# A fused attention and gated-MLP kernel: clears moved behind the key maximum, an own buffer for the warm-up products, and a fixed table of order and banks

## The chip, the cores and the metric

The kernel runs on one core of a Trainium2 chip. A core has engines that run side by side, each through its own list of instructions in order: TensorE (matmuls and transposes, PE in the profile), ScalarE (ACT), VectorE (DVE), GpSimd (POOL), and SyncE (SP), which issues the transfers. They wait for each other through semaphores. The metric is the device time of one execution in microseconds, the median of the runs; lower is better.

## The reference

One sequence of 2048 rows of 640 numbers goes through a layer norm. From there two branches run: attention with 32 heads of 20 numbers each, and a gated MLP block that shifts quarters of its hidden features along the sequence. The result is the input plus the attention output times the SiLU of the other branch.

```python
def _A_ref(x, wqkv, wo):            # H = 32, Dh = 20
    ...
    scores = jnp.einsum("bhqd,bhkd->bhqk", q, k) * (Dh ** -0.5)
    p = _softmax(scores, axis=-1)
    o = jnp.einsum("bhqk,bhkd->bhqd", p, v)
    ...
def _B_ref(x, w1, w2, w3, w4):
    h = _gelu(_layernorm(x, axis=-1) @ w1)
    ...
    hs = jnp.concatenate([g0, g1, g2, g3], axis=-1) @ w2
    x1 = x + hs
    h2 = _gelu(_layernorm(x1, axis=-1) @ w3) @ w4
    return x1 + h2
x = A_x
xn = _layernorm(x, axis=-1)
s = _A_ref(xn, A_wqkv, A_wo)
g = _silu(_B_ref(xn, B_w1, B_w2, B_w3, B_w4))
return x + s * g
```

## The kernel before

**A program that plans itself.** The code does not write instructions in their final order. It makes a list of tasks: each names an engine, an estimated duration, what it reads and writes, and sometimes a due time. A planner then orders the tasks of each engine. In the kernel before it is a list scheduler (`schedule`): it steps through an estimated time line and picks, for each engine, the ready task with the earliest derived due time. It also hands out PSUM banks and buffers for exponentials (`acq`, `rel`, `choose`). The due times come from `DUE`, a table of offsets. From the order, `plan_sync` works out the semaphore waits, and `emit` writes each engine's list. On the chip each list is fixed and is run strictly in order.

**The opening.** The input is loaded in eight transfers of two 128-row tiles. Each of the 16 tiles is normalised: for some, VectorE computes the statistics (`bn_stats`, L1014, two halves of 320 for each tile), for others ScalarE does so (`ln_tiles_act`, L1046 and L1048). GpSimd takes the power -0.5 of the variance (L1024, L1060). The normalisation itself runs on VectorE or GpSimd (L1029) or, for the tiles with statistics from ScalarE, on ScalarE (L1071) or GpSimd (L1067). `LNA` says how many tiles of each eight go to ScalarE, `POOLN` which tiles GpSimd normalises. TensorE transposes the normalised tiles (L1120), four tiles and one of five column chunks at a time; VectorE (L1130) or ScalarE (L1127) copies the result to `xnT`. `TRA` lists the copies that ScalarE does.

Ahead of that, TensorE runs warm-up products whose result isn't used (`warm`, L981), so that its clock is at full speed when the work comes. They read `QM`, a buffer of query chunks that GpSimd clears first (L947). `NPF` says how many: 34 tasks of four products at the start, 8 more after the first transposes.

**The softmax bound.** Instead of the row maximum, the kernel subtracts a bound for each query. For the first quad of heads it is made in the opening (`prep`): for each of four chunks, the keys are projected, VectorE takes the largest absolute key (L1193), and ScalarE copies the keys out (L1196). From the maximum over all chunks (L1199) a small matrix `Mq` is filled (L1201). The absolute queries (copied at L1165, the sign bit cleared by a bit operation at L1166) times this matrix give the shift (L1174), which is added to the queries, and the result is copied out (L1181, L1185). Only then can the first scores be computed. GpSimd clears the second halves of `KT` and `QT` (L973, L974) for later quads.

**The body.** Eight quads of four heads, and in each of them four chunks of 512 queries, are worked through; for each there are 16 key tiles of 128. TensorE computes scores (L1524 over rows of the array, L1542 over columns), ScalarE exponentiates 1024 of them per partition at a time (L1589), and TensorE multiplies with the values (L1382). To relieve ScalarE, some pairs of key tiles, the *blocks*, are split: half of each tile's heads is exponentiated by VectorE through integer arithmetic on bit patterns (L1616 makes the exponent bits, L1507 makes three shifted copies), which costs TensorE four value products in place of one (L1516). `ND` gives the number of blocks for each quad and chunk, `NR` the key tiles whose scores use rows of the array. Between the scores lie the projections of later heads, the values, and the whole MLP branch (all through `mm_tile`, L797), with evictions on VectorE.

**The tail.** The last chunk of the last quad is done in halves (`last_half`), then the output projection, the product with the gate, and the stores follow.

Of the kernel before, what the change touches and what calls it, by code (L numbers as in the profile page):

```python
# [6 lines left out]
def _log(*a, **k):  # L7
    pass
# [4 lines left out]
class _Heap:  # L13

    @staticmethod
    def heappush(h, item):
        h.append(item)
        i = len(h) - 1
        while i > 0:
            p = (i - 1) >> 1  # L20
            if h[i] < h[p]:
                h[i], h[p] = h[p], h[i]
                i = p
            else:
                break

    @staticmethod
    def heappop(h):
        last = h.pop()
        if not h:  # L30
            return last
        top = h[0]
        h[0] = last
        n = len(h)
        i = 0
        while True:
            l = 2 * i + 1
            r = l + 1
            m = i
            if l < n and h[l] < h[m]:  # L40
                m = l
            if r < n and h[r] < h[m]:
                m = r
            if m == i:
                break
            h[i], h[m] = h[m], h[i]
            i = m
        return top

    @staticmethod  # L50
    def heapify(h):
        n = len(h)
        for s in range(n // 2 - 1, -1, -1):
            i = s
            while True:
                l = 2 * i + 1
                r = l + 1
                m = i
                if l < n and h[l] < h[m]:
                    m = l  # L60
                if r < n and h[r] < h[m]:
                    m = r
                if m == i:
                    break
                h[i], h[m] = h[m], h[i]
                i = m


heapq = _Heap

# [6 lines left out]
class Task:  # L91
    __slots__ = ("id", "eng", "dur", "fn", "reads", "writes", "due", "name",
                 "preds", "succs", "order_preds", "start", "finish", "seq",
                 "signals", "dma_sem", "lat", "pos", "npred", "prio", "is_dma",
                 "acq", "rel", "stream", "sidx", "cls", "nbytes", "mode", "ndma", "tile", "dlat")

    def __init__(self, tid, eng, dur, fn, reads, writes, due, name, lat, is_dma):
# [28 lines left out]
        self.dlat = 0.0  # L126


class Planner:
# [87 lines left out]
    def task(self, eng, dur, fn, reads=(), writes=(), due=None, name="", lat=0.0,  # L217
             is_dma=False, acq=None, rel=None, stream=None, after=(), cls=0, nbytes=0, mode=0, ndma=1, tile=None, dlat=0.0):
# [6 lines left out]
        t.tile = tile  # L225
        t.dlat = dlat
        if is_dma and nbytes:
            t.lat = self.dma_lat0 + nbytes / self.dma_bw + dlat
# [55 lines left out]
    def avail(self, pstate, a):  # L284

        ps = pstate[self.home[a[0]]]
        return min(max(ps[i][0] for i in banks) for _, banks in self.kinds[a[0]])

    def choose(self, pstate, kind, now):

        ps = pstate[self.home[kind]]
        best = None
        for rank, banks in self.kinds[kind]:
            ft = max(ps[i][0] for i in banks)
            if ft <= now + 1e-9 and (best is None or (rank, ft) < best[0]):
                best = ((rank, ft), banks)
        return best[1]

    def schedule(self, verbose=False):
        tasks = self.tasks  # L300
        n = len(tasks)
        for t in tasks:
            t.succs = []
        for t in tasks:
            for p in t.preds:
                tasks[p].succs.append((t.id, True))
            for p in t.order_preds:
                tasks[p].succs.append((t.id, False))
        horizon = 0.0
        for t in tasks:  # L310
            if t.due is not None:
                horizon = max(horizon, t.due)
        for t in reversed(tasks):
            d = t.due if t.due is not None else INF
            for (sid, sync) in t.succs:
                s = tasks[sid]
                sd = s.prio - s.dur - (SYNC_LAT[t.eng] if sync else 0.0) - t.lat
                if sd < d:
                    d = sd
            if d == INF:  # L320
                d = horizon + 1e6
            t.prio = d
        first = {}
        for t in tasks:
            if t.tile is not None:
                first.setdefault(t.tile, t.prio)
                t.prio = min(t.prio, first[t.tile])
        for t in tasks:
            if t.eng == "dve" and t.rel is not None:
                t.cls = -1  # L330
            if t.cls and t.eng in self.strict_engines:
                t.prio = t.prio + t.cls * self.cls_penalty
        npred = [len(t.preds) + len(t.order_preds) for t in tasks]
        ready_time = [0.0] * n
        eng_free = {e: 0.0 for e in ENGINES}
        ready = {e: [] for e in ENGINES}
        for t in tasks:
            if npred[t.id] == 0:
                heapq.heappush(ready[t.eng], (t.prio, t.id))
# [3 lines left out]
        dma_free = 0.0  # L343
        done = 0
        pe_mode = 0
        WINDOW = 48
        while done < n:
            best = None
            for e in ENGINES:
                h = ready[e]  # L350
                if not h:
                    continue
                tf = eng_free[e]
                tmp = []
                cand = None
                early = None
                saved = set()
                k = 0
                while h and k < WINDOW:
                    item = heapq.heappop(h)  # L360
                    tmp.append(item)
                    k += 1
                    t = tasks[item[1]]
                    rt = ready_time[item[1]]
                    if t.acq:
                        if any(a[0] in saved for a in t.acq):
                            continue
                        r0 = rt
                        for a in t.acq:
                            ft = self.avail(pstate, a)  # L370
                            if ft > rt:
                                rt = ft
                            if ft > tf and a[0] in self.saves and r0 <= tf + self.reserve and (self.hard or rt < INF):
                                saved.add(self.saves[a[0]])
                    if rt <= tf + 1e-9:
                        if cand is None:
                            cand = (tf, item)
                        if e != "pe" or not pe_mode or t.mode == pe_mode:
                            if t.mode == pe_mode:
                                cand = (tf, item)  # L380
                            break
                        continue
                    if cand is None and t.cls < 0 and (t.acq or e != "pe") and rt <= tf + self.hold.get(e, 0.0):
                        cand = (rt, item)
                        break
                    if early is None or rt < early[0]:
                        early = (rt, item)
# [214 lines left out]
class Handle:  # L602
    _n = 0
# [1413 lines left out]
```

## Time and profile before

| what | value |
|---|---|
| time, median of 3 runs | 864.06 us (862.28 to 864.19) |
| profiled span | 862.9 us |
| TensorE busy | 813.6 us |
| ScalarE busy | 818.7 us |
| VectorE busy | 723.7 us |
| GpSimd busy | 41.9 us |
| first exponential starts | 39.44 us |
| granted clock of TensorE, mean | 0.996 |

The busy time of an engine counts the instructions it runs, not its waits. In the profile a line such as L1589 stands for the place in the code that made the instruction; a helper like `mm_tile` (L797) stands for many callers. In the groups of instructions, the number after `|` is the busy time and the mean duration of one, and after the second `|` stands the idle time of the engine just ahead of them, with what ended most of it. The chain of waits follows the work that ended last, back from the end of the program, and gives start, duration and place of each piece.

### The profile page before, as it was taken

The page shows a single profiled execution, that of the slowest core. Times are in us where ns is not written, and L with a number is a line of the kernel's source. Part 1 is how long each engine was busy: PE and PEld are TensorE (multiplying, and loading weights), DVE is VectorE, ACT ScalarE, POOL GpSimd, SP SyncE. Part 2 cuts the span into 40 slices and gives each one's busy share as a digit, 9 for nine tenths or more (in the row PEclk, how much of TensorE's full clock was granted, in tenths as well). Part 3 has the DMA queues.
Part 4 walks back from the last instruction along what each step waited for, and adds up shares of the span by engine and source line. Part 5 has one row for each costly group of instructions (what it writes and reads, how often), then busy time and mean ns, then how long its engine had stood idle before and what let it go on. Part 6 is the DMA issues. An engine that isn't in the chain of part 4 may idle for free.

```text
span 862.9 us, 33979 instructions
## 1 busy us (share of the span) xinstructions
PE 813.6 (94%) x15538; PEld 362.4 (42%) x15538; DVE 723.7 (84%) x977; ACT 818.7 (95%) x855; POOL 41.9 (5%) x74
## 2 busy tenths in 40 slices
PE   6899999999999999999999999999997999999996
PEld 3433433334434533343344444344333444534474
DVE  6728987998998899989887799997986788999765
ACT  6599999999999999999999999999999999999986
POOL 8500000000000100000000000000000000000000
PEclk9999999999999999999999999999999999999999
DMA  7003333313010022223225021323221103032331
GB/s 229 17 9 84 94 114 85 118 28 99 17 56 26 25 59 66 63 74 80 56 69 131 23 71 29 87 64 87 63 55 49 48 25 72 25 103 66 89 114 64
DMA packets 86479, 58.99 MB, mean 68 GB/s; under 512 B 53056, under 2 KB 77840, under 8 KB 86336
## 3 DMA queue, kind: packets, MB, share of 16 engines
q1 hardware_dynamic: 86336, 56.82, 24.3%
q8 instruction: 122, 2.00, 1.0%
q14 instruction: 21, 0.17, 0.1%
HBM read 42.10 MB, written 10.63 MB: 61 GB/s over the span
## 4 chain that ended last, share of the span: by engine, by line
PE 51%; ACT 36%; DVE 10%; DMA 1%; issue 1%; POOL 1%; SPq 0%; DVEq 0%; POOLq 0%
ACT arena L1589 31%; PE psum L797 17%; PE psum L1542 12%; PE psum L1524 7%; PE psum L1382 6%; PE psum L1516 5%; DVE arena L1616 4%; ACT arena L1959 2%; DVE arena L1507 2%; PE psum L981 1%; ACT arena L1888 1%; DMA shifts<-arena 1%; ACT arena L1566 1%; PE psum L1120 1%; DVE arena L1260 1%
## 5 line engine op out<-in xcount | busy, mean ns | idle before, releaser
L1589 ACT ACTIVATE arena<-psum 128x1024 bf16<-128x1024 f32 x786 | 736.2, 1035 | 20.3 <-PE psum L1524 12.9
L797 PE MATMUL psum<-arena 128*32 128x320 bf16 (+1 forms) x5952 | 351.6, 333 | 5.4 <-DVE arena L1216 2.2
L1616 DVE TENSOR_SCALAR arena<-psum 128x1024 uint16<-128x1024 f32 (+1 forms) x222 | 267.8, 1207 | 44.3 <-PE psum L1524 42.8
L1542 PE MATMUL psum<-arena 128*32 128x512 bf16 x3664 | 278.9, 381 | 10.9 <-ACT arena L1589 9.2
L797 PEld LDWEIGHTS psum<-arena 128*32 128x32 bf16 x5952 | 148.0, 96 | 133.2 <-issue 28.8
L1507 DVE TENSOR_SCALAR arena<-arena 128x4096 uint16<-128x4096 uint16 (+1 forms) x174 | 197.4, 1160 | 1.0
L1382 PE MATMUL psum<-arena 128*22 128x512 bf16 x1544 | 148.2, 381 | 2.9 <-ACT arena L1589 2.6
L1516 PE MATMUL psum<-arena 128*22 128x512 bf16 x1760 | 141.2, 380 | 0.7 <-DVE arena L1507 0.4
L1542 PEld LDWEIGHTS psum<-arena 128*32 128x32 bf16 x3664 | 80.0, 95 | 102.4 <-ACT arena L1589 70.4
L1524 PE MATMUL psum<-arena 32*128 32x512 bf16 x1068 | 111.1, 384 | 12.1 <-ACT arena L1589 6.0
L1524 PEld LDWEIGHTS psum<-arena 32*128 32x128 bf16 x1068 | 28.3, 91 | 121.2 <-ACT arena L1589 74.0
L1382 PEld LDWEIGHTS psum<-arena 128*22 128x22 bf16 x1544 | 38.5, 91 | 60.1 <-issue 16.8
L1516 PEld LDWEIGHTS psum<-arena 128*22 128x22 bf16 x1760 | 42.9, 92 | 48.1 <-issue 8.4
L1260 DVE CAST arena<-psum 128x512 bf16<-128x512 f32 x40 | 27.2, 684 | 17.4 <-PE psum L797 17.3
L1955 DVE CAST arena<-psum 128x512 bf16<-128x512 f32 x48 | 32.8, 684 | 4.4 <-PE psum L797 4.4
L1739 DVE SCALAR_TENSOR_TENSOR arena<-psum,arena 128x320 bf16<-128x320 f32 x32 | 15.5, 486 | 18.9 <-PE psum L797 18.9
L1321 DVE CAST arena<-psum 128x320 bf16<-128x320 f32 x32 | 15.4, 488 | 18.2 <-PE psum L797 18.0
L1014 DVE BATCH_NORM_STATS2 arena<-arena 128x6 f32<-128x320 bf16 x52 | 23.0, 478 | 2.7 <-DMA arena<-in_A_x_dram 2.6
L1959 ACT ACTIVATE arena<-arena 128x12288 bf16<-128x12288 bf16 x2 | 20.9, 10446 | 0.0
L1651 DVE COPY arena<-psum 128x512 f32<-128x512 f32 x28 | 19.1, 683 | 0.7 <-PE psum L1516 0.6
L981 PE MATMUL psum<-arena 128*32 128x512 bf16 x168 | 12.8, 463 | 7.3 <-POOL arena L947 6.4
L1664 DVE TENSOR_TENSOR arena<-arena 128x512 bf16<-128x512 f32 x28 | 19.1, 681 | 0.5 <-DMA arena<-recips 0.5
(119 smaller groups left out, 352.1 us busy)
## 6 DMA issues: line engine op xcount, KB each, us to landing
arena<-in_B_w_dram SPq DMA_DIRECT2D x48, 160.0 KB, 2.7
arena<-recips SPq DMA_DIRECT2D x28, 256.0 KB
arena<-arena SPq DMA_DIRECT2D x124, 32.0 KB, 1.9
arena<-in_B_w_dram SPq DMA_DIRECT2D x4, 960.0 KB, 7.0
arena<-in_A_x_dram SPq DMA_DIRECT2D x8, 320.0 KB, 5.3
arena<-in_A_x_dram SPq DMA_DIRECT2D x16, 160.0 KB, 2.4
out_dram<-arena SPq DMA_DIRECT2D x16, 160.0 KB, 1.8
arena<-keys SPq DMA_DIRECT2D x28, 80.0 KB
```

The source lines that it names most:

```text
L797: ins = e.matmul(pb[32 * c:32 * c + 32, 0:N], lhsT(k, c), rhs(k, c), start=(k == 0), stop=(stop and k == nk - 1), tile_position=(0, 32 * c))
L1014: lambda e, li=li, n=n, hh=hh: e.bn_stats(st[:, li, 6 * hh:6 * hh + 6], xn[:, n, hD * hh:hD * hh + hD]),
L1260: T("dve", c_dve(512), lambda e, h=h, c=c: e.tensor_copy(KS[:, 512 * c:512 * c + 512], self.wbank(h)[:, 0:512]), reads=[wa], writes=[A("KS ...
L1382: ins = e.matmul(pb[32 * i:32 * i + 22, 0:512], VA[:, ql, kts[i // 2], i, :], PT[:, slots[i // 2][0].slot, 512 * (i % 2):512 * (i % 2) + 512],
L1507: T("dve", c_dve(w, "4x"), lambda e, v=v, dst=dst: e.tensor_scalar(dst, U[:, ub, 0:w], EXP_B[v], None, op0=ALU.add), reads=halves, writes= ...
L1516: ins = e.matmul(pb[32 * i:32 * i + 22, 0:512], wv, dst[:, at:at + 512].bitcast(BF16), start=first, stop=final, tile_position=(0, 32 * i))
L1524: return e.matmul(out, self.KT[32 * i:32 * i + 32, b, 128 * kt:128 * kt + 128], self.QT[32 * i:32 * i + 32, b, 512 * qc:512 * qc + 512], s ...
L1542: ins = e.matmul(out[32 * c:32 * c + 32, :], self.KT[:, b, 128 * kt + 32 * c:128 * kt + 32 * c + 32], self.QM[:, gb, 2 * a + jj, :], start ...
L1589: lambda e: e.activation(self.PT[:, hp.slot, :], self.psum[:, 512 * hs.slot:512 * hs.slot + 1024], AF.Exp, scale=cfg.scale),
L1616: ins = e.tensor_scalar(U[:, ub, 1024 * at + 512 * k:1024 * at + 512 * k + w], self.psum[:, 512 * hd.slots[k]:512 * hd.slots[k] + w], a_ex ...
L1955: T("dve", c_dve(512), lambda e, h=h, fc=fc, i=i: e.tensor_copy(GT[:, i, fc, :], self.wbank(h)[:, 0:512]), reads=[wa], writes=at, name=f"g ...
L1959: T("act", 2750 + c_act(2 * FC * 512), lambda e: e.activation(GT[:, :, :, :], GT[:, :, :, :], AF.Gelu_apprx_tanh), reads=gta, writes=gta, ...
```

## The change

Its purpose is to shorten the opening and to give each engine a better order.

1. The warm-up products read a small buffer `wz`, a part of `Ob` that VectorE clears, in place of `QM`. There are 36 tasks, and none of the second kind.
2. The clears of `QM`, of the second halves of `KT` and `QT`, of the second half's value columns, and the long power of the MLP branch (`r2`) now come behind the key maximum `MX`.
3. When GpSimd normalises a tile whose statistics VectorE made, it multiplies and adds (with -mean times the inverse deviation, made by a small VectorE instruction) where it subtracted and multiplied. The tiles that go to GpSimd and ScalarE change.
4. The list scheduler is taken out. `follow` reads a fixed table in which each entry names the next task and, where it needs a buffer, which banks; estimated times are kept only to work out the waits. Tasks that use GpSimd's port are marked `lock`. The rule that scores may run only a few tiles ahead (`turns`) is taken out.
5. `ND` is changed in three places; many `DUE` values and some others that only the old scheduler used change as well.

```diff
-    def schedule(self, verbose=False):
+    def follow(self, table):
...
+        while at < len(table):
+            t = tasks[len(code) * code[table[at]] + code[table[at + 1]]]
+            at += 2
...
             for kind, *handles in t.acq:
                 home = self.home[kind]
                 ps = pstate[home]
-                banks = self.choose(pstate, kind, st)
+                banks = self.kinds[kind][code[table[at]]][1]
+                at += 1
...
-        self.POOLN = [0, 9, 14]
+        self.POOLN = [2, 4, 7, 15]
...
-        self.LNA = [3, 3]
-        self.VAFTER = 6
-        self.NPF = [34, 8]
-        self.TRA = [1, 2, 3, 4, 8, 13, 17, 18]
+        self.LNA = [3, 2]
+        self.VAFTER = 16
+        self.NPF = [36, 0]
+        self.TRA = [1, 2, 4, 5, 6, 7, 8, 9, 13, 16]
...
         self.ND = (
             [0, 4, 4, 3],
             [4, 4, 4, 4],
-            [3, 2, 4, 4],
+            [3, 1, 4, 4],
...
-            [4, 4, 2, 3])
+            [4, 3, 2, 4])
...
-        T("pool", 3500, lambda e: e.memset(self.QM[:, :, :, :], 0.0), writes=[A("QM", k) for k in range(2)], name="qm0", due=-40000.0)
...
+        self.wz = self.Ob[:, 0:256].bitcast(BF16)
+        T("dve", 200, lambda e: e.memset(self.wz[:, :], 0.0), writes=[A("Ob")], name="wz0", due=-50000.0)
...
-            ins = e.matmul(self.bank(self.PVB)[32 * c:32 * c + 32, 0:512], self.QM[:, 0, 0, 0:32], self.QM[:, 1, 0, 0:512], start=True, stop=True,
+            ins = e.matmul(self.bank(self.PVB)[32 * c:32 * c + 32, 0:512], self.wz[:, 0:32], self.wz[:, 0:512], start=True, stop=True,
...
+            if ve_out and n in cfg.POOLN:
+                T("dve", 120, lambda e, li=li: e.scalar_tensor_tensor(nb[:, li:li + 1], mv[:, li, 0:1], -1.0, rs[:, li:li + 1], op0=ALU.mult, op1=ALU.mult),
...
+                T("pool", 1000, lambda e, li=li, n=n: e.tensor_scalar(dst_of(n), xn[:, n, :], rs[:, li:li + 1], nb[:, li:li + 1], op0=ALU.mult, op1=ALU.add),
...
+        after = [A("MX", 0)]
+        T("pool", 3840, lambda e: e.memset(self.QM[:, :, :, :], 0.0), reads=after, writes=[A("QM", k) for k in range(2)], name="qm0", due=self.at(8))
+        T("pool", 1810, lambda e: e.memset(self.KT[:, 1, :], 0.0), reads=after, writes=[A("KT0")], name="kt0", due=self.at(60))
+        T("pool", 1810, lambda e: e.memset(self.QT[:, 1, :], 0.0), reads=after, writes=[A("QT0")], name="qt0", due=self.at(60))
...
-          reads=self.turns() + [("gate",), A("KT", b, kt // 4)] + ([A("QT", b, qc), A("QTa", b, qc)] if gb is None else [A("QM", gb)]),
-          writes=[sa, ("turn", self.step)], name=f"sc{self.step}", mode=int(gb is None), cls=-1, acq=("S", hs))
+          reads=[("gate",), A("KT", b, kt // 4)] + ([A("QT", b, qc), A("QTa", b, qc)] if gb is None else [A("QM", gb)]),
+          writes=[sa], name=f"sc{self.step}", mode=int(gb is None), cls=-1, acq=("S", hs))
...
-          reads=[A("tv", 1), A("mh2")], writes=[A("R2")], name="r2")
+          reads=[A("tv", 1), A("mh2"), A("MX", 0)], writes=[A("R2")], name="r2")
```

The table itself is a string of 87 lines; two characters name a task, and one more a set of banks.

## The prediction

> **What bounds the kernel now.** I read the page first: two engines are busy nearly all the time.
>
> ```profile
> PE 813.6 (94%) x15538; PEld 362.4 (42%) x15538; DVE 723.7 (84%) x977; ACT 818.7 (95%) x855; POOL 41.9 (5%) x74
> PE   6899999999999999999999999999997999999996
> ACT  6599999999999999999999999999999999999986
> POOL 8500000000000100000000000000000000000000
> L1589 ACT ACTIVATE arena<-psum 128x1024 bf16<-128x1024 f32 x786 | 736.2, 1035 | 20.3 <-PE psum L1524 12.9
> L1616 DVE TENSOR_SCALAR arena<-psum 128x1024 uint16<-128x1024 f32 (+1 forms) x222 | 267.8, 1207 | 44.3 <-PE psum L1524 42.8
> ```
>
> ScalarE carries 786 exponentials of 1.035 us. The tenths show it below nine only in the first two slices (43 us) and the last. So the time is an opening before the first exponential, a body paced by ScalarE, and a tail. The windows view, cut at the first exponential (39.4) and after the last (853.6), sizes the body; its columns are PE, PEld, DVE, ACT and POOL busy, each with a count.
>
> ```profile
> 39.40:853.60 814.20, 782.29 (x14788) 345.29 (x14789) 689.43 (x879) 794.35 (x811) 12.79 (x26) 1.00 0.24 65
> ```
>
> ScalarE works 794.35 of 814.20 us: 19.85 us of idle is all that a better order can win there. The tail is 862.9 - 853.6 = 9.3 us. The opening is the loosest part, so I read its chain of waits, with the timeline for the durations of single instructions.
>
> ```profile
> 1.72 1.23 POOL arena L1314
> 2.95 3.42 POOL arena L947
> 6.42 10.43 PE psum L981 x127
> 16.85 1.18 PE psum L1120 x78
> ...
> 32.66 0.70 DVE arena L1165
> 33.38 2.95 DVE arena L1166
> 36.33 0.60 DVE arena L1193
> 36.96 0.17 DVE arena L1199
> 37.15 0.40 DVE arena L1201
> 37.55 0.04 issue
> 37.60 0.61 PE psum L1174 x8
> ```
>
> The clear of QM (L947) holds the warm-up products (L981) until 6.42, and these hold the transposes (L1120) until 16.85. Later one VectorE bit operation (L1166) takes 2.95 us; the line's own view gives 293/293/2948 ns for its three executions. The GpSimd timeline shows what lies over it:
>
> ```profile
> 31.37 1.81 POOL L973 MEMSET arena<- 128x2048 bf16 x1
> 33.11 1.81 POOL L974 MEMSET arena<- 128x2048 bf16 x1
> 34.86 0.11 POOL L963 MEMSET arena<- 128x10 bf16 x1
> 34.90 0.10 POOL L1010 MEMSET arena<- 128x4 f32 x1
> 34.94 1.25 POOL L1314 MEMSET arena<- 128x256 bf16 x1
> ```
>
> It ends at 36.33, just after the last of these (36.19). The last key maximum, the row shift, the first query chunk and all attention wait for it.
>
> **What the Trainium skill says.** "SBUF — State Buffer", section "Who interferes with whom": VectorE's second port pair is GpSimd's only one and is locked exclusively. The trace agrees: 2.95 us against 0.29. "TensorE: Matmul & The Clock Gate", section "Part 1: The HAM clock gate": the array runs at half rate until a window of about 3.4 us has been busy. The trace agrees in kind: the windows view counts 32, 36 and 64 warm-up products in three successive stretches of 3 us, so the fast rate came after some 6 us. "PSUM — Partial Sum Buffer", section "Engine vs sequencer instructions": matmuls start in program order. So a transpose stands behind every product ahead of it; the chain above shows just that.
>
> **The change, part by part.**
>
> *Warm-up.* The products read `wz`, cleared by VectorE at the head of its list. A clear of the same engine (L968) takes 0.48 us and starts at 0.99; so the products start at 1.5, not 6.4. Decoding the head of the table by the diff's rules gives the order: 31 of 36 warm-up tasks (four products each) stand ahead of the first transpose. From the windows above, 68 products took the slow 6.0 us; the other 56 at 3.0/64 = 0.047 us take 2.6, so they end at 10.1. If the slow spell lasts longer, the whole old rate of 10.43/136 = 0.077 gives 9.5 us and 11.0. The transposes of the first group then wait for its normalised tiles. In VectorE's list 14 half-tile statistics stand ahead of them: 14 x 0.415 (four take 1.66) = 5.8 us from the first data at 3.94; five aggregates at 0.11 and a dozen small instructions at 0.08 add 1.5; one normalisation adds 0.4: 11.7. I take 12.0 for the first transpose: 4.85 us earlier than 16.85.
>
> *From the first transpose to the shift product.* Before: 37.60 - 16.85 = 20.75 us. The clears of QM, KT and QT, the second half's VA clears and the long power (2.92 us) now wait for the key maximum, so L1166 gets its 0.29 us back: 2.66 off. Warm-up products in this stretch fall from 32 to 20 (0.061 each in the chain): 0.7 off. One value tile of 20 products at 0.045 goes behind the shift: 0.9 off. That leaves 16.5. VectorE gets one more tile of statistics (0.83 + 0.11) and one more to normalise (0.40), ScalarE loses two statistics and two normalisations (5.1 us by 0.73 + 0.19 and 0.93 each, less the overlap) and gains two evictions of 0.60; GpSimd takes four normalisations, by multiply-add 1.00 us each (L1067) where subtract-multiply took 2.50 (L1029). These lie beside TensorE's 16 us. I add 1.0 for waits in a new order: 17.5, between 16.5 and 20. Shift product at 29.5; the old 1.84 us from it to the first exponential gives 31.3, against 39.44: 8.1 us gained, bounds 5 and 9.
>
> *What the moved clears may hold up.* QM 3.84, the power 2.92 and two clears of 1.81 now run for 10.4 us behind the maximum, and the bit operations of query chunks 2 and 3 stand on VectorE beside them. Behind those are the evictions on VectorE, the shift products on TensorE, and behind these the next scores. The table puts shift 2 ahead of the eighth score tile and shift 3 ahead of the eleventh, so ScalarE has about 7 and 10 us of exponentials in hand. I cost it at nothing, hidden by these; at worst 3 us.
>
> *Fewer blocks.* `ND` drops one block of two key tiles in quad 2, chunk 1, and one in quad 7, chunk 1; the other changed entry, the last chunk of the last quad, isn't read, since that chunk goes to `last_half`. Each takes two 1024-wide halves from VectorE and gives ScalarE two exponentials, 2.07 us; in quad 7 one key tile falls on a wide row (1.89 for two). Sum: 2.07 + 1.88 = 3.95 us more on ScalarE. VectorE loses 4 x 1.22 and six pieces go from 4096 to 2048 wide (1.215 to 0.686): 8 us less. TensorE hardly changes.
>
> *Order and banks.* The table replaces the list scheduler and the limit on scores ahead of the exponentials. It costs no time by itself; it acts on the 19.85 us of ScalarE idle, of which 12.9 are waits for row scores (L1524). Nothing in the trace prices it. Bounds: 6 us, a third left; 20, nothing won; more if the fixed order stalls. I take 14: some waits go, as VectorE is relieved where blocks go, and the end of each engine's queue is strict. The tail's code is the same: 9.3.
>
> **Sum.** 31.3 + (794.35 + 3.95) + 14 + 9.3 = 852.9 us of span; the median of the runs lies 864.06 - 862.9 = 1.2 above the profiled span: 854.1 us.
>
> **Rivals.**
> - *Only the opening.* The body keeps 19.9 us of idle and carries 3.95 more: 31.3 + 798.3 + 19.9 + 9.3 + 1.2 = 860.0. For it: all that the profile explains lies in the opening, and TensorE, busy 782 of 814 us, leaves little room. Against it: blocks were handed to ScalarE, which makes sense only where it waited.
> - *The body wins much.* Idle falls to 7: 847.1. For it: 62 waits of VectorE for row scores (42.8 us) and 32 of ScalarE show slack in the order. Against it: TensorE is then at 97% of the body.
> - *Slower: the fixed order stalls.* In-order queues on three engines, with a wait wherever an estimate was off: the opening gets to 35 (VectorE locked out anew behind the maximum), idle rises to 33: 35 + 798.3 + 33 + 9.3 + 1.2 = 876.8. For it: a wait of TensorE holds everything behind it. Against it: the order of before was fixed too when it ran, and lost only 20 us.
>
> **How the numbers follow.** My forecast (idle 10 to 17) has 0.47, only the opening 0.26, the large gain 0.17, the stall 0.10. The forecast is the likeliest: 854.1. Faster by over 0.3% means below 861.5. The first and third lie below it, the second does so for most of its part; part of the stall ends between: faster 0.90, same 0.04, slower 0.06. The range leaves out the far ends of the large gain and of the stall: 845.5 to 861.5.
>
> **What would show it.** Right: TensorE's first product near 1.5, the first transpose near 12, no instruction of L1166's kind at 2.9 us ahead of the shift product, the first exponential at 30 to 33, 788 exponentials of 1024, ScalarE's idle in the body 10 to 17. Wrong: transposes that still wait until 15 or more, which would make the normalised tiles the bound; a long bit operation just behind the maximum with TensorE waiting for it; or idle over 20, which would say that the table gives back the opening's gain.

## The result and the profile after

The changed kernel takes 866.42 us (median of four runs, 866.21 to 867.08) against 863.58 for the kernel before beside it: a ratio of 1.0036, with a 95% interval of 1.0019 to 1.0054. It is slower, by about 3 us; the forecast was 854.1. The page of the kernel after, with the lines that answer to those shown of before (busy time, ScalarE's tenths, the exponentials; L1423 is L1589 of before):

```profile
PE 821.2 (95%) x15526; PEld 360.1 (42%) x15526; DVE 723.1 (84%) x997; ACT 817.9 (95%) x854; POOL 38.4 (4%) x75
ACT  7599979999999999999999999999999999999996
L1423 ACT ACTIVATE arena<-psum 128x1024 bf16<-128x1024 f32 x788 | 735.3, 1039 | 24.3 <-PE psum L1363 13.2
```

788 exponentials stand where 786 stood, and ScalarE's busy time hardly changes (817.9 us for 818.7). Its tenths have a 7 in the sixth slice (108 to 130 us) that wasn't there before, and its idle time ahead of the exponentials is 24.3 us where it was 20.3. The body, from the first exponential to the end of the last, in the windows view (columns as in the prediction), of the kernel before and of the kernel after:

```profile
39.44:854.44 815.00, 782.79 (x14794) 345.45 (x14790) 689.75 (x880) 795.19 (x811) 12.79 (x26) 1.00 0.24 65
37.23:856.75 819.52, 790.47 (x14826) 344.43 (x14820) 689.40 (x897) 796.18 (x814) 17.71 (x30) 1.00 0.24 64
```

ScalarE works 796.18 of 819.52 us and is idle for 23.34, where before it was idle for 19.81. So the first exponential comes 2.2 us earlier than before (37.23 against 39.44), and the body is 4.5 us longer. Why so little in the opening? The chain of waits of the kernel after, its first 45 us (start, duration, place):

```profile
1.80 5.06 DMA arena<-in_A_x_dram
...
12.57 0.37 DVE arena L861
12.98 0.30 PE psum L952 x4
...
29.54 0.70 DVE arena L1025
30.26 0.17 DVE arena L1031
30.46 3.58 DVE arena L1033
34.08 1.04 PE psum L1006 x4
35.12 1.71 PE psum L626 x8
36.83 0.36 PE psum L1363 x4
```

The transposes (L952) start at 12.98, 3.9 us earlier than before, and the warm-up products are no longer ahead of them: what they wait for is a normalised tile (L861). The key maximum (L1031) ends at 30.43. Then one VectorE instruction stands in the way for 3.58 us: L1033, which fills `Mq`, and which took 0.40 in the chain of before. The timeline of the kernel after shows what is beside it (start, duration, engine, line, shapes; in brackets the idle time before it and what ended that):

```profile
30.46 3.57 DVE L1033 TENSOR_SCALAR arena<-arena 128x4 bf16<-128x4 f32 x1
30.48 3.51 POOL L1036 MEMSET arena<- 128x4096 bf16 x1 [6.60 <-DVE arena L1031]
33.96 2.90 POOL L1670 TENSOR_TENSOR arena<-arena 128x16 f32<-128x16 f32 x1
34.08 1.04 PE L1006 MATMUL psum<-arena 128*32 128x512 bf16 x8 [3.51 <-DVE arena L1033]
```

The maximum releases two instructions at once: the fill of 128x4 numbers on VectorE, and the moved clear of `QM` (L1036) on GpSimd. The fill starts on paper 0.02 us ahead, and ends 0.04 us after the clear. That is the long bit operation of before in a new place, and it fits what the Trainium skill says in "SBUF — State Buffer", section "Who interferes with whom", of an exclusive lock on the port pair that the two share. TensorE idles 3.51 us, and the eight shift products (L1006) then take 1.04 us. The windows view of the next four microseconds, where the last three columns are the granted clock, the share of the DMA engines and GB/s, says why:

```profile
34.00:38.00 4.00, 3.92 (x46) 1.31 (x48) 1.05 (x3) 1.55 (x2) 4.00 (x2) 0.64 0.04 10
```

The granted clock is 0.64. The skill's page "TensorE: Matmul & The Clock Gate", section "Part 1: The HAM clock gate", has the clock fall after an idle window of about 3.4 us. The gap of 3.51 us would fit that, but in the same trace the clock also falls behind gaps of 2.16 us (10.82 to 12.98, ahead of the first transpose) and of 1.65 us (from 115.52), so less was enough here:

```profile
12.98:16.39 3.41, 2.71 (x84) 2.18 (x88) 2.80 (x10) 1.63 (x3) 1.47 (x5) 0.50 1.07 352
118.79:122.20 3.41, 3.41 (x32) 0.90 (x34) 2.31 (x3) 2.81 (x3) 0.00 (x0) 0.50 0.55 143
```

The first of the two falls on the transposes. Sixty of them take 1.82 us in the kernel after, and 1.06 in e1 below, where the clock stayed at 1 after a gap of 2.25 us:

```profile
13.49 1.82 PE L952 MATMUL psum<-arena 128*32 128x128 bf16 x60
12.90 1.06 PE L964 MATMUL psum<-arena 128*32 128x128 bf16 x60
```

So the warm-up now ends too early for its purpose: its last product ahead of the transposes ends 2.16 us before the first of them.

A second, smaller loss lies in the slice with the 7. The chain of waits of the kernel after in that stretch:

```profile
104.94 2.86 DMA recips<-arena
...
107.81 0.59 SPq L1496
...
108.45 6.75 DMA queries<-arena
...
115.22 0.04 DVE arena L1064
```

SyncE's list is in order too. A store of queries is issued behind a broadcast of the reciprocals (L1496), which waited for these to land; the store takes 6.75 us, and VectorE, which takes the sign bits off the stored queries (L1064), waits 2.5 us for it. Shortly after, ScalarE has its two longest gaps: 1.57 us at 116.1 and 2.55 at 123.7.

### The profile page after: what moved, and what is told of

Its sections match the earlier page's. It is cut to its first block, busy times and chain, and to the rows that moved or that the text cites. A ratio compares the mean times of both kernels' runs of the same rounds, so it can differ in the third digit from the quotient of the medians.

```text
span 865.4 us, 33986 instructions
## 1 busy us (share of the span) xinstructions
PE 821.2 (95%) x15526; PEld 360.1 (42%) x15526; DVE 723.1 (84%) x997; ACT 817.9 (95%) x854; POOL 38.4 (4%) x75
## 4 chain that ended last, share of the span: by engine, by line
ACT 43%; PE 40%; DVE 13%; DMA 3%; issue 1%; SPq 0%; DVEq 0%
ACT arena L1423 40%; PE psum L626 15%; PE psum L1381 10%; PE psum L1355 5%; PE psum L1363 4%; DVE arena L1450 4%; PE psum L1221 4%; DVE arena L1346 3%; ACT arena L1722 1%; DVE arena L1098 1%; ACT arena L1405 1%; DVE arena L1052 1%; DMA queries<-arena 1%; DVE arena L841 1%; ACT arena L1809 1%
## 5 line engine op out<-in xcount | busy, mean ns | idle before, releaser
L1423 ACT ACTIVATE arena<-psum 128x1024 bf16<-128x1024 f32 x788 | 735.3, 1039 | 24.3 <-PE psum L1363 13.2
L626 PE MATMUL psum<-arena 128*32 128x320 bf16 (+1 forms) x5952 | 364.9, 334 | 4.0 <-DVE arena L1160 1.2
L1450 DVE TENSOR_SCALAR arena<-psum 128x1024 uint16<-128x1024 f32 (+1 forms) x237 | 264.4, 1123 | 43.9 <-PE psum L1363 42.5
L1381 PE MATMUL psum<-arena 128*32 128x512 bf16 x3712 | 283.0, 382 | 7.9 <-ACT arena L1423 6.7
L1346 DVE TENSOR_SCALAR arena<-arena 128x4096 uint16<-128x4096 uint16 (+1 forms) x174 | 194.6, 1143 | 1.2
L1355 PE MATMUL psum<-arena 128*22 128x512 bf16 x1728 | 150.2, 384 | 4.3 <-DVE arena L1346 4.0
L1221 PE MATMUL psum<-arena 128*22 128x512 bf16 x1552 | 149.1, 381 | 2.6 <-ACT arena L1423 1.5
L1750 DVE TENSOR_TENSOR arena<-psum,arena 128x320 bf16<-128x320 f32 x32 | 15.1, 483 | 8.0 <-PE psum L626 7.8
L1804 DVE TENSOR_TENSOR arena<-psum,arena 128x320 bf16<-128x320 f32 x32 | 15.6, 486 | 5.5 <-PE psum L626 5.1
```

Of the source, the lines that this page charges most:

```text
L626: ins = e.matmul(pb[32 * c:32 * c + 32, 0:N], lhsT(k, c), rhs(k, c), start=(k == 0), stop=(stop and k == nk - 1), tile_position=(0, 32 * c))
L1221: ins = e.matmul(pb[32 * i:32 * i + 22, 0:512], VA[:, ql, kts[i // 2], i, :], PT[:, slots[i // 2][0].slot, 512 * (i % 2):512 * (i % 2) + 512],
L1346: T("dve", c_dve(w, "4x"), lambda e, v=v, dst=dst: e.tensor_scalar(dst, U[:, ub, 0:w], EXP_B[v], None, op0=ALU.add), reads=halves, writes= ...
L1355: ins = e.matmul(pb[32 * i:32 * i + 22, 0:512], wv, dst[:, at:at + 512].bitcast(BF16), start=first, stop=final, tile_position=(0, 32 * i))
L1381: ins = e.matmul(out[32 * c:32 * c + 32, :], self.KT[:, b, 128 * kt + 32 * c:128 * kt + 32 * c + 32], self.QM[:, gb, 2 * a + jj, :], start ...
L1423: lambda e: e.activation(self.PT[:, hp.slot, :], self.psum[:, 512 * hs.slot:512 * hs.slot + 1024], AF.Exp, scale=cfg.scale),
```

## The experiments

The theory from this profile: the opening is lost to the port just behind the maximum, and the body's start to the store. The rivals: the late fill only hides a wait that would end there anyway; the loss is in the table's order or in the handed-over blocks.

All kernels of the first group are the kernel after, with the table read into rows first, so that an entry can be moved (`MOVE`) or a wait added (`EXTRA`: the second waits for the first); nothing else changes unless it is shown, and their lines stand 12 higher than those of the kernel after (the fill is L1045, the exponentials L1435). Names of entries: `mq_` is the fill of `Mq`, `qm0` the clear of `QM`, `qm0_1` the first transfer into it, `aq_3` the last of the opening's bit operations, `kt0` and `qt0` the clears of `KT` and `QT`, `r2` the long power, `dk0_0` the query store, `r10_1` the broadcast.

```diff
+        for first, then in EXTRA:
+            tasks[name[then]].preds.add(name[first])
...
+        for what, where, ref in MOVE:
+            row = next(r for r in rows if r[0] == name[what])
+            rows.remove(row)
+            k = next(i for i, r in enumerate(rows) if r[0] == name[ref])
+            rows.insert(k + (where == "behind"), row)
```

Results in us; the ratio is to the kernel before on the same chip (e1 to e4 ran on one chip, e5 to e8 and b2 on a second, e9, b1 and b3 on a third). The first exponential and the body are those of one profiled run, which can lie some way off the median (e7 865.83 for 862.85, b3 868.60 for 866.75); so a microsecond between two bodies says little by itself.

| kernel | first exponential | body | median | ratio, 95% interval |
|---|---|---|---|---|
| before | 39.44 | 815.0 | 863.4 to 864.0 | 1 |
| after | 37.23 | 819.5 | 866.42 | 1.0036 (1.0019 to 1.0054) |
| e1, fill ahead of the clear | 31.76 | 817.4 | 859.61 | 0.9951 (0.9932 to 0.9970) |
| e2, store ahead | 35.96 | 819.0 | 865.05 | 1.0009 (0.9996 to 1.0021) |
| e3, both | 32.07 | 815.7 | 859.04 | 0.9944 (0.9925 to 0.9962) |
| e4, clears behind the bit operations | 31.82 | 816.8 | 859.97 | 0.9954 (0.9938 to 0.9971) |
| e5, fill on ScalarE | 33.58 | 816.0 | 859.74 | 0.9956 (0.9942 to 0.9969) |
| e7, old warm-up | 34.01 | 821.8 | 862.85 | 0.9995 (0.9978 to 1.0011) |
| e8, old normalisation | 35.49 | 816.8 | 862.34 | 0.9992 (0.9981 to 1.0004) |
| e9, e3 with the value products earlier | 32.86 | 817.6 | 858.29 | 0.9935 (0.9916 to 0.9954) |
| b1, before with late clears | 35.03 | 816.4 | 863.18 | 0.9987 (0.9969 to 1.0006) |
| b2, before with the new opening's clears and warm-up | 35.95 | 815.2 | 860.97 | 0.9975 (0.9960 to 0.9991) |
| b3, before with the new blocks | 38.94 | 819.2 | 866.75 | 1.0033 (1.0015 to 1.0052) |

### e1: the clear waits for the fill

```diff
+EXTRA = [("mq_", "qm0")]
```

> The changed kernel with one more wait: the clear of QM on GpSimd starts only when VectorE has filled Mq, so the two no longer start together behind the key maximum. Port theory: the filling of Mq falls from 3.57 us to below 0.5, TensorE doesn't sit idle for 3.5 us ahead of the shift product and so keeps its full rate, the first exponential moves from 37.2 to about 32.5 us, and the time falls from 866.4 by some 4.7 to about 861.7. Rival (the body sets its own pace, bound to transfers and to the other engines): the first exponential moves as far, but the total stays within 1.5 us of 866.4.

The timeline of e1 around the maximum:

```profile
29.43 0.16 DVE L1043 TENSOR_REDUCE arena<-arena 128x1 f32<-128x4 f32 x1
29.63 0.24 DVE L1045 TENSOR_SCALAR arena<-arena 128x4 bf16<-128x4 f32 x1
29.92 0.62 PE L1018 MATMUL psum<-arena 128*32 128x512 bf16 x8 [0.17 <-DVE arena L1045]
29.92 3.51 POOL L1048 MEMSET arena<- 128x4096 bf16 x1 [7.06 <-DVE arena L1045]
31.76 1.02 ACT L1435 ACTIVATE arena<-psum 128x1024 bf16<-128x1024 f32 x1 [0.61 <-PE psum L1375]
```

The same clear, of the same 3.51 us, 0.29 us later: the fill takes 0.24 us, TensorE idles 0.17, the shift products take 0.62, and the first exponential comes at 31.76, 5.5 us earlier than in the kernel after. One wait makes the kernel faster than both, and shows the theory for the opening. The gain is 2 us more than expected, since the body is shorter too. The bit operations, 1.99 and 1.04 us in the kernel after, take at most 0.28 here.

The changed planner does know of the port: the fill and the clear are both marked `lock`, and in its estimated times a marked task begins only when the marked one ahead of it in the table has ended. But the mark makes no wait. On the chip nothing keeps the clear behind the fill, and both start when the maximum is there.

### e5: the fill on ScalarE

e1 also moves the clear. If what matters is VectorE's port and not the clear's time as such, the fill is quick on another engine while the clear runs.

```diff
-        T("dve", 90, lambda e: e.tensor_scalar(Mq[:, :, 20], self.maskn[:, 0:4], self.MX[:, 0:1], None, op0=ALU.mult),
+        T("act", 250, lambda e: e.activation(Mq[:, :, 20], self.maskn[:, 0:4], AF.Copy, scale=self.MX[:, 0:1]),
```

> The changed kernel with Mq filled by ScalarE instead of VectorE; the clear of QM starts behind the key maximum as in the change, beside it. Port theory: ScalarE shares no port with GpSimd, so the filling takes 0.2 to 0.3 us although the clear runs; it stands behind the last key copy on ScalarE, so the shift product starts near 31.5, the first exponential near 33, and the time is about 861. Rival (the clear or its start delays whatever follows the key maximum, whichever engine does it): the shift product stays near 34 and the time near 866.

The timeline of e5, in which the maximum (L1043) ends at 30.87:

```profile
30.92 3.51 POOL L1048 MEMSET arena<- 128x4096 bf16 x1 [6.59 <-DVE arena L1043]
31.39 0.30 ACT L1045 ACTIVATE arena<-arena 128x4 bf16<-128x4 f32 x1
31.74 0.61 PE L1018 MATMUL psum<-arena 128*32 128x512 bf16 x8 [0.73 <-ACT arena L1045]
```

The fill takes 0.30 us in the middle of the clear. So it is VectorE's access that the clear held up. The median is that of e1 (on another chip). In the profiled run the first exponential comes 1.8 us later than in e1's: the transposes start 0.7 us later (13.33 for 12.61), the shift products wait 0.5 us longer behind the maximum, and the granted clock is 0.50 from 14.90 to 18.32, behind the gap ahead of the transposes.

### e4: the clears behind all bit operations

```diff
+EXTRA = [("mq_", "r2"), ("aq_3", "qm0")]
+MOVE = [("qm0", "behind", "aq_3"), ("qm0_1", "behind", "qm0")]
```

> The changed kernel with the clears of QM, KT, QT and the second half's VA put behind the last bit operation of the queries (chunk 3), and the long power behind Mq; the first copy into QM moves behind its clear. Port theory: no bit operation of the opening takes over 0.4 us, where the changed kernel has 1.99 and 1.04; the first exponential is at about 32.5 as with the one wait more, and the 1 us of ScalarE idle at 43 to 48 us goes: about 861. Rival (GpSimd's long power holds the port too): a bit operation beside the power takes over 2 us.

The first exponential is where e1 has it (31.82), no bit operation is over 0.29 us, and the time is that of e1. The bit operations were quick in e1 already, so there was nothing left for this to win.

### e2 and e3: the query store ahead of the broadcast, alone and with e1

```diff
+MOVE = [("dk0_0", "ahead", "r10_1")]
```

> The changed kernel with one transfer put elsewhere: the store of the first stack's queries is issued just ahead of the broadcast of the second chunk's reciprocals, not just behind it. Store theory: VectorE's wait of 2.5 us for this store at 112.7 to 115.2 goes, ScalarE's idle time between 88 and 140 us falls from 6.4 to about 2.5 us, and the time falls by some 3.5 to about 863. Rival (the store isn't the limit, the projections are late by themselves): the idle time in this stretch stays above 5 us and the time within 1 us of 866.4. A broadcast that now lands later could hold the normalisation of that chunk instead.

> Both edits together. If the opening and the store are two separate losses, the gains add: about 858. If the order has slack at neither place, 865 to 867. If the earlier opening only makes the body wait longer at the store, it equals the better one of the two, about 862.

VectorE no longer waits for the store, which takes 3.9 us in e2 and e3 for 6.75 in the kernel after. In the first 100 us of the body ScalarE is idle for 7.4 us in the kernel after and 5.4 in e2, for 5.2 in e1 and 4.3 in e3; one gap of 2.46 us stays. The gain of e3 is 0.6 us beside e1 (within both intervals); that of e2 beside the kernel after is 1.4 us by the medians, and the two ratios' intervals overlap. The 3.5 us that I expected aren't there. e3 is the kernel after with both repairs. Its windows view over the body:

```profile
32.07:847.80 815.73, 789.05 (x14826) 344.31 (x14822) 687.08 (x897) 795.78 (x814) 22.56 (x32) 1.00 0.24 65
```

Idle is 19.95 us of 815.73: what the kernel before had, not the 14 of the forecast. In the other kernels in which no instruction of the opening is held up (e1, e4, e5, e8, e9) it lies between 20.4 and 21.5.

### e9: the first value products of the next chunk earlier

The gap that stays in e3 is a wait for the first value product of a new chunk, which waits for the copy of the accumulated outputs and then stands behind 28 products of a projection. e9 puts both ahead.

```diff
+MOVE = [("dk0_0", "ahead", "r10_1"), ("ob0_2", "ahead", "u0_3_7"), ("pv0_3_b0", "ahead", "s1_1_1_1")]
```

> The version with both repairs (859.0), and the stall of 2.46 us on ScalarE that is left near 115 us taken on: the copy of the accumulated head outputs (L1497 there) goes ahead of the last exponent-bits operation on VectorE, and the first value product of the next chunk goes ahead of seven groups of projection products on TensorE. If the order alone makes the stall, it falls to about 1 us and the time to about 857.8. Rival (TensorE is full in this stretch, its chain shows no gap): the idle time appears again within the next 20 us, time 858.5 to 859.5.

The gap of 2.46 us becomes two, of 1.38 and 0.98 us, 2 us apart. TensorE is busy for 39.7 of the 40 us around it (92 to 132, in e3 and in e9), so it is TensorE's work that is short there, and the order only says which exponential waits. 858.29 us is the lowest of all, but it can't be told from e3.

### e7 and e8: two parts of the opening put back

e7 lets the warm-up products read `QM` again, cleared ahead of them, and keeps the other clears behind the fill. e8 is e1 with the old form of normalisation on GpSimd.

```diff
-            ins = e.matmul(self.bank(self.PVB)[32 * c:32 * c + 32, 0:512], self.wz[:, 0:32], self.wz[:, 0:512], start=True, stop=True,
+            ins = e.matmul(self.bank(self.PVB)[32 * c:32 * c + 32, 0:512], self.QM[:, 0, 0, 0:32], self.QM[:, 1, 0, 0:512], start=True, stop=True,
...
-        T("pool", 3840, lambda e: e.memset(self.QM[:, :, :, :], 0.0), reads=after, writes=[A("QM", k) for k in range(2)], name="qm0", due=self.at(8))
+        T("pool", 3840, lambda e: e.memset(self.QM[:, :, :, :], 0.0), reads=[], writes=[A("QM", k) for k in range(2)], name="qm0", due=self.at(8))
...
+EXTRA = [("mq_", "kt0"), ("mq_", "r2"), ("qm0", "warm0")]
+MOVE = [("qm0", "ahead", "warm0")]
```

> The version with Mq ahead of the clears (859.6), but the warm-up products read QM again, which GpSimd clears among its first instructions. If the warm-up's start sets the opening, the first product comes near 5.3, the first transpose near 15.5 in place of 13.0, the first exponential near 34.3 and the time near 862.2. Rival (the normalised tiles set it, the warm-up hides behind them): first transpose at 13 to 14, time within 1 us of 859.6.

The products start at 5.14, the transposes at 15.18 where e1 has 12.61, the first exponential comes 2.3 us later than in e1. That is about the worth of the small buffer in the opening; where the clock falls at the transposes, as in e9 (32.86), less is left of it. The total mixes it with a side effect: a bit operation took 3.45 us beside the clears of `KT` and `QT`, which start at another time here, ScalarE then idled 2.43 us at 39.8, and the granted clock was 0.50 from 41.49 to 48.32. The profiled run is 3.0 us above the median, so that its body is no measure of the kernel.

```diff
-                T("pool", 1000, lambda e, li=li, n=n: e.tensor_scalar(dst_of(n), xn[:, n, :], rs[:, li:li + 1], nb[:, li:li + 1], op0=ALU.mult, op1=ALU.add),
+                T("pool", 1000, lambda e, li=li, n=n: e.tensor_scalar(dst_of(n), xn[:, n, :], mv[:, li, 0:1], rs[:, li:li + 1], op0=ALU.subtract, op1=ALU.mult),
```

> The version with Mq ahead of the clears (859.6), but GpSimd normalises tiles 2 and 4 by subtract-multiply again. Each takes 2.5 us where multiply-add took 0.88. Only the one of tile 2 has the power for tiles 0 and 1 right behind it on GpSimd: these tiles, the first transposes and the first exponential come about 1.6 us later, and the time is about 861.2. Rival (hidden behind the warm-up products and VectorE): within 0.5 us of 859.6.

GpSimd's timeline in e8, and in e1 at the same place in its list:

```profile
11.12 2.52 POOL L869 TENSOR_SCALAR arena<-arena 128x640 bf16<-128x640 bf16 x1 [0.41 <-DVE arena L899]
13.62 0.71 POOL L863 TENSOR_TENSOR arena<-arena 128x2 f32<-128x2 f32 x1
```

```profile
10.43 0.89 POOL L869 TENSOR_SCALAR arena<-arena 128x640 bf16<-128x640 bf16 x1 [0.43 <-DVE arena L899]
11.29 0.69 POOL L863 TENSOR_TENSOR arena<-arena 128x2 f32<-128x2 f32 x1
```

The power for other tiles (L863) stands behind the normalisation in GpSimd's list. It starts 2.3 us later, and the transposes too (14.86 against 12.61). Of that, the 1.6 us that I had expected are the longer normalisation; it also starts 0.7 us later, because the input for VectorE's third half-tile landed later in this run (its statistics start at 7.21, in e1 at 6.52). The first exponential is 3.7 us later: TensorE was idle for 3.41 us ahead of the transposes, and the granted clock was 0.50 from 14.24 to 21.06. Beside e5 on the same chip the median is 2.6 us higher; what of the 1.0 us above the expected 1.6 is due to the clock isn't shown.

### b1, b2, b3: parts of the change in the kernel before

The order that the list scheduler of before finds is kept and replayed, with entries moved as above (b1, b2); in b3 only `ND` is changed and the scheduler plans anew. b1 moves the clears of `KT`, `QT` and the value columns behind the bit operations; b2 moves that of `QM` as well and warms up from `wz`.

```diff
+EXTRA = [("aq_3", "kt0")]
+MOVE = [("kt0", "behind", "aq_3"), ("qt0", "behind", "kt0"), ("VA1_1", "behind", "qt0"), ("VA0_1", "behind", "VA1_1"), ("kt1", "behind", "qt0")]
```

> The kernel before in its own order, with one edit: the clears of KT, QT and the second half's VA come behind the last bit operation of the queries (QM is cleared first, as before, for the warm-up). The opening's bit operation falls from 2.95 to 0.3 us, the first exponential comes at 36.8, and the time is about 2.6 lower, near 861. Rival (the body takes the gain back at its first transfers): within 1 us of the kernel before.

In the profiled run the bit operation takes 0.29 us and the first exponential comes at 35.03; but the runs scatter from 858.3 to 866.4, the median is only 0.8 us lower, and the ratio's interval includes 1.

```diff
-            ins = e.matmul(self.bank(self.PVB)[32 * c:32 * c + 32, 0:512], self.QM[:, 0, 0, 0:32], self.QM[:, 1, 0, 0:512], start=True, stop=True,
+            ins = e.matmul(self.bank(self.PVB)[32 * c:32 * c + 32, 0:512], self.wz[:, 0:32], self.wz[:, 0:512], start=True, stop=True,
...
+MOVE += [("qm0", "behind", "kt1"), ("qm0_1", "behind", "qm0")]
```

> The kernel before in its own order of all engines, with two edits of the opening alone: the warm-up products read the small buffer, and the clears of KT, QT, QM and the second half's VA come behind the last bit operation of the queries. The opening's bit operation falls from 2.95 to 0.3 us (2.66 off), and the transposes start near 13.4, when GpSimd has normalised tile 0, not at 16.85 (3.4 off): first exponential near 33.4. If the body of the old order is as good as that of the table, the time is about 864.0 - 6.0 = 858, no worse than the two repairs of the table together (859.0). If the table's body is worth something by itself, this one is slower than 859 by as much.

The first exponential is at 35.95 (expected 33.4), the body is that of before, and 2.4 us are won: these two parts help without any of the rest. The transposes do start early (13.90), but then wait for later tiles until 16.09, and the granted clock is 0.50 from 16.34 to 19.75.

```diff
-            [3, 2, 4, 4],
+            [3, 1, 4, 4],
...
-            [4, 4, 2, 3])
+            [4, 3, 2, 4])
```

> The kernel before with ND of the change alone, order again by the list scheduler (which orders the body anew from the second quad on). ScalarE gets two exponentials of 1024 and one wide one more in place of two narrow ones. If the handed-over work sets the time, it is 2 to 4 us slower than before, 866 to 868; if ScalarE fills idle time with it, within 1 us; if VectorE was the limit there, 1 to 3 us faster.

The windows view of b3 over its body:

```profile
38.94:858.16 819.22, 784.22 (x14806) 346.94 (x14801) 683.78 (x876) 799.19 (x814) 12.20 (x26) 1.00 0.24 65
```

ScalarE's work grows by 4.00 us over before (3.95 forecast), idle stays at 20.03, and the body grows by 4.2: in the old order the handed-over blocks cost all they weigh in this run. By the medians b3 is 2.8 us slower than before (1.3 to 4.5 by the interval). Beside b3, e3 has the same 814 instructions of ScalarE in the body and the same idle time, and 3.4 us less work. It lies in the 788 exponentials of 1024 (b3, then e3):

```profile
L1589 ACT ACTIVATE arena<-psum 128x1024 bf16<-128x1024 f32 x788 | 738.3, 1035 | 19.5 <-PE psum L1524 11.7
L1435 ACT ACTIVATE arena<-psum 128x1024 bf16<-128x1024 f32 x788 | 734.9, 1039 | 19.8 <-PE psum L1375 9.4
```

Each lasts no less (1.035 and 1.039 us on the mean), but busy time counts overlapping ones once, so in the table's order more of them overlap the one before. This holds beyond one run: the nine kernels with the table show 795.6 to 796.2 us of work in the body.

## Why the prediction was wrong

By its own steps, with the miss of the span: 865.4 - 852.9 = 12.5 us.

- **Warm-up: right.** First product at 1.84 (1.5), transposes at 12.98 (12.0) and waiting for normalised tiles, as forecast. 1.0 us of the miss. The forecast's own numbers (products until 10.1, transposes from 12.0) held an idle stretch of 1.9 us for TensorE, which it costed at nothing; in five of the nine profiled kernels that warm up from `wz` the granted clock fell within 2.5 us of the first transpose (after, e5, e8, e9, b2), and in none of the four that warm up from `QM`. In the kernel after this is worth about half a microsecond: from the first transpose to the end of the maximum it takes 17.45 us, and e1 16.98.
- **From the first transpose to the shift product: right but for what follows.** 17.5 us were forecast; the kernel after shows 21.10, e1, in which the fill isn't held up, 17.31. From the shift product to the first exponential 1.84 us were forecast; after shows 3.15, e1 shows 1.84. The 1.0 us for waits in the first sum was a guess, so that it comes out is in part luck.
- **"What the moved clears may hold up": this step failed.** It named the bit operations of query chunks 2 and 3, which do have exponentials in hand, and cost the clears at nothing. (With the value columns, which its 10.4 us leave out, the clears and the power run for 12.4 us, from 30.48 to 42.90.) It passed over the instruction on VectorE that starts with them, the fill of `Mq`, which has nothing in hand: shift, queries, scores and the first exponential all stand behind it. The fill's excess of 3.3 us (3.57 for 0.24 in e1) and the slower stretch behind it, 1.3 us (3.15 for 1.84), are nearly all of the 4.9 us lost behind the transposes. The prediction had the key: 2.95 us for one bit operation beside the old clears. It asked which instruction was long in the trace, and not which VectorE instruction would be next to a clear after the move. The "slower" rival did name VectorE "locked out anew behind the maximum", as 35 for the first exponential; it was 37.23. Of its signs of being wrong two came: a long VectorE instruction just behind the maximum with TensorE waiting for it, though the fill and not a bit operation, and idle over 20.
- **"Order and banks": this step failed too.** It took idle from 19.85 to 14. With both repairs (e3) idle is 19.95. The other 3.4 us of the 23.34 in the kernel after lie in the first 200 us of the body. In its first 100 us, e1 has 2.2 us less than the kernel after, and e3 0.8 less than e1, which is what the store's move is worth there. e1's 21.53 over the whole body holds 0.9 more from another place, a gap of 2.21 us at 658 (1.28 in e3): just ahead of it the granted clock was 0.50 for 6.8 us, and for 3.4 in e3. The order's gain that was forecast in idle time isn't there; what e3 has over b3 is in ScalarE's busy time.
- **Fewer blocks: right in the term, wrong in the sum.** 788 exponentials and +4.0 us of work in b3; VectorE is relieved of 6.0 us there (689.75 to 683.78), not 8. In the kernel after, ScalarE's work in the body is 796.18, not 798.3, through the overlap just told.
- **Sum of the miss:** opening +5.9, of it 1.0 up to the transposes and 4.9 behind them; idle +9.3; ScalarE's work -2.1; tail 8.65 for 9.3, -0.65. That makes 12.5. The forecast had set the end of the last exponential at 853.6; it is at 854.44. From the marks used here before has 795.19 of work and a tail of 8.46, so that the work falls short of the forecast by 3.0 us and the tail grows by 0.2.
- **The rivals.** "Only the opening" (860.0: first exponential 31.3, work 798.3, idle 19.9) is nearly what the repaired kernel shows: e3 has 32.07, 795.78, 19.95 and 859.04. As handed over, the change gives the opening back at the port. "The body wins much" isn't seen in any run. Of "the fixed order stalls" the place was right and the size not: idle 23.34 for 33.

What stays open: the old list scheduler over all of the other changes wasn't tried, so what the table alone is worth is known only by difference (e3 against b3: the profiled bodies are 3.5 us apart, the medians 7.7, of which the openings make 6.9 and so leave 0.8). How much the store costs, 0.6 or 1.4 us, can't be told apart. That the gap ahead of the transposes makes the clock fall is likely and not shown: e7, whose products end 0.4 us ahead of them, has no such fall, but e1 to e4 had gaps of 1.5 to 2.3 us and none either. No run has the small buffer and more products.

## What to carry to other kernels

When work is moved to a later event, list what else that event releases on every engine that shares a resource with it, and ask of each how much work is in hand behind it; here a 3.5 us clear and a 0.24 us instruction on the path started together, and one wait between them is worth 6.8 us (866.42 to 859.61). A move off one critical instruction isn't costed at nothing until its new neighbours are named. An order that a planner keeps only in its estimated times isn't kept on the chip, unless a wait goes with it. Warm-up products that end before the work comes may lose a part of what they were for: here the last one ended 2.16 us early, and the first transposes ran at half the clock. An engine that is busy for 97% has two margins, its idle time and how closely its instructions follow each other, and only the first is seen as idle.

## What the hardware showed unexpectedly

- A VectorE instruction that was held up stayed held up through the clears that followed closely: in the kernel after, a bit operation of VectorE begun at 39.69, under one clear (38.55 to 40.35), lasted 1.99 us, to 41.68, through the next clear (40.28 to 41.54). It takes 0.28 when free. In e7 one begun at 36.48 lasted 3.45 us, through three clears. The fill in the kernel after began 0.02 us ahead of the clear by the trace, and was yet the one held up.
- Not all that GpSimd runs holds VectorE up, nor all that VectorE runs is held up: in e1 a bit operation at 34.23 took 0.28 us under the long power (33.40 to 36.30), and a copy out of PSUM at 32.32 took its usual 0.69 under the clear of `QM` (29.92 to 33.43). What was held up was read and written in SBUF, under a clear.
- GpSimd normalises a tile of 128x640 in 0.88 to 0.89 us as multiply and add, and in 2.51 to 2.52 us as subtract and multiply (e1 and e8).
- The same store of queries took 6.75 us issued just behind a broadcast of 256 KB (kernel after; 6.38 in e1), and 3.9 just ahead of it (e2 and e3).
- The granted clock of TensorE fell to one half for 3.41 us or for twice that (6.83 in e7 and, near 650, in e1). A gap alone didn't decide it: 1.65 us was enough at one place in the kernel after, and 2.25 us was not in e1. In e2 it fell at 34.07, when TensorE had worked again for 0.76 us behind a gap of 3.51. The three falls in the first 130 us of the kernel after, at 12.98, 33.46 and 118.79, lie 20.48 and 85.33 us apart, which is 6 and 25 times 3.41 to within 0.1 us.
